# Sliding-window attention in five score units instead of six, with a relaid dense schedule

## The chip, the cores and the metric

The kernel runs on one core of a Trainium2 chip. The metric is device time in microseconds of one execution, as the median of several. A profile of one execution by the hardware profiler goes with it; its span runs from the first to the last instruction, and the execution's own time is a little longer than the span.

The engines are named as the profile names them: PE is TensorE (matrix products), PEld its weight loads, DVE is VectorE, ACT is ScalarE, POOL is GpSimd, and SP issues the DMA transfers from one queue (SPq).

## What is computed

A transformer block over 2048 tokens of width 512. A conditioning vector `c` gives six modulation rows (shift, scale and gate, twice). The first half is attention with 32 heads of width 16, in which a query sees its own and the 255 keys before it. The second half mixes tokens with an MLP over the sequence axis.

```python
mod = (silu(c) @ w_mod)            # six rows: sa, ca, ga, sb, cb, gb
h = layernorm(x) * (1 + ca) + sa
qkv = h @ wqkv                     # 32 heads, Dh = 16
scores = q @ k.T * Dh ** -0.5
mask = (0 <= i - j) & (i - j < 256)
o = softmax(where(mask, scores, -1e9)) @ v
x = x + ga * (o @ wo)
h = layernorm(x) * (1 + cb) + sb
u = gelu(einsum('sd,sf->df', layernorm(h), w1) + b1)   # S=2048, F=1792
x = x + gb * (u @ w2 + b2).T
```

## The kernel before

Tokens are cut into 16 blocks of 128, four blocks make a tile group (`tg` = 0 to 3), and the work has three parts: a short start up to the first scores, an attention loop over the four tile groups, and an MLP part in which TensorE works through W1, the GELU and W2.

**The attention loop.** Heads are taken four at a time (`hs` = 0 to 7; `g8 = hs // 2`, and `par` tells even from odd heads). TensorE runs four heads side by side in four 32-row strips of its array. One such set and one tile group needs 512 queries against up to 256 keys behind each of them, in blocks of 128 keys. A block of keys is fully or partly seen by 3 blocks of queries, so 12 blocks of 128 columns stand in 3 units of 512 columns (`UNITS`). A unit has four score banks of 512 columns, two `pss` tiles of two banks each. A loop step (`u`) does, in the order in which the code emits it:

- the exponential of the unit's first `pss` tile on ScalarE (`emit_exp(u, 0)`, L517), 1024 columns into bf16 `et`
- on TensorE the scores and masks of the next unit (`emit_scores(u + 1)`, L494 and L505); a mask is a small matmul that adds a huge negative number to what must not be seen. Three `pss` tiles exist, so its second tile takes the place of the one that the exponential just read
- on TensorE one "dense group" from a plan (`plan`), if the unit has one: Q, K or V projections of 4 matmuls of 512 columns, transposes of the normalised input, output projections, modulation rows or part of W1. It goes to one PSUM bank, the only buffer of `ps_dn`
- the exponential of the second tile (`emit_exp(u, 1)`)
- on VectorE pieces of LayerNorm and normalisation work from a list (`run_dve`), of which as many are taken as a planned budget per unit allows (2.0 us less what is queued), and then the emptying of the dense group
- on TensorE the products P·V of the unit before (`emit_av(u - 1)`, L533) into `po`, one bank. After the third unit of a set VectorE transposes `po` into `t2` (L547). Per pair of sets a reciprocal, a product and a transpose back follow (L556, L557, L564).

Every engine works in its own order of instructions; a standing instruction holds all behind it on its engine.

**K.** A projected K of a `g8` is cast into one buffer `ks` (L305), which `kspool` holds once. Eight small transfers (L315, 16 KB each) then spread its rows over two zeroed tiles, one per parity; the other parity's rows stay zero. The zeros come by DMA (`zeros`, L197). The next cast into `ks` waits until the eight transfers have landed. In the first tile group the first two `g8` are masked by VectorE instead.

**The plan.** In a unit number `ul` within the tile group (0 to 23), V is at 0 to 2, K of `g8` = 2 at 4 (5 in the first tile group), K of `g8` = 3 at 9, the next group's transposes at 11 to 14 and its first K's at 18 and 22. The budget's costs stand in the code beside each piece.

**Around it.** All of w_mod and the zeros are issued by SP's queue at the start; w1's first twelve row tiles are loaded in the second half of tile group 1 (from unit 16 on), the last four, and all of w2, after the loop. LayerNorm's two elementwise products (L591, L594) and the quotient (L557) run on VectorE.

Of the kernel before, what the change touches and what calls it, by code (L numbers as in the profile page):

```python
# [8 lines left out]
DT = mybir.dt  # L9
ACT = mybir.ActivationFunctionType  # L10
ALU = mybir.AluOpType
# [12 lines left out]
SCORE_SCALE = DH ** -0.5  # L24


@with_exitstack
def kernel(
# [61 lines left out]
    opool = ctx.enter_context(tc.tile_pool(name="opool", bufs=3))  # L90
# [31 lines left out]
    seed = modw.tile([32, 4 * P], DT.bfloat16, name="seed")  # L122
    seed_q = modw.tile([32, 2, 64], DT.bfloat16, name="seed_q")
    mask_k = const.tile([P, 4, P], DT.bfloat16, name="mask_k")
# [4 lines left out]
    def build_masks():  # L129
        v = nc.vector  # L130
        v.tensor_copy(
            out=spread[:].rearrange("p (a b) -> p a b", a=4),
            in_=identity[0:32, 0:32].unsqueeze(1).to_broadcast([32, 4, 32]),
        )
        bands = seed[:].rearrange("p (t x) -> p t x", t=2)
        for kind, (e0, e1) in enumerate(((-47, 0), (14, -33))):
            for lo in (0, 192):
                band = bands[:, kind, lo : lo + 64].rearrange("p (r s) -> p r s", s=2)
                v.memset(band[:, :, 0:1], 2.0 ** e0)
                v.memset(band[:, :, 1:2], 2.0 ** e1)  # L140
        v.memset(seed[:, 64:128], 2.0 ** 47)
        v.memset(seed[:, 128:192], 0.0)
        v.memset(seed[:, 320:384], 0.0)
        v.memset(seed[:, 384:448], 2.0 ** 14)
        for kind, (e0, e1) in enumerate(((14, -33), (0, 47))):
            q = seed_q[:, kind, :].rearrange("p (r s) -> p r s", s=2)
            v.memset(q[:, :, 0:1], -(2.0 ** e0))
            v.memset(q[:, :, 1:2], -(2.0 ** e1))

        def select(ap, pattern, base, cm, fill):  # L150
            nc.gpsimd.affine_select(
                out=ap, in_=ap, pattern=pattern, compare_op=ALU.is_ge, fill=fill, base=base, channel_multiplier=cm,
            )

        for lo in (0, 192):
            band = bands[:, :, lo : lo + 64]
            select(band, [[0, 2], [1, 64]], 0, -2, 0.0)
            select(band, [[0, 2], [-1, 64]], 1, 2, 0.0)
        select(seed[:, 64:128], [[0, 64]], -31, 1, 0.0)
        select(seed[:, 384:448], [[0, 64]], 0, -1, 0.0)  # L160
        select(seed_q[:, 0, :], [[1, 64]], 0, -2, -(2.0 ** 61))
        select(seed_q[:, 0, :], [[-1, 64]], 1, 2, 0.0)
        select(seed_q[:, 1, :], [[1, 64]], 0, -2, 0.0)
        select(seed_q[:, 1, :], [[-1, 64]], 1, 2, -(2.0 ** 47))
# [10 lines left out]
    epool = tc.alloc_tile_pool(name="epool", bufs=3)  # L175
# [20 lines left out]
    def zeros(r, g0=0):  # L196
        dma.dma_start(  # L197
            out=Kring[r][:, g0:].rearrange("p g n t -> p (g n) t"),
            in_=zero[:].unsqueeze(1).to_broadcast([P, 2 * (ND - g0), 4 * P]),
        )  # L200

    zeros(0, 2)
    zeros(1)
    for v in (2, 4, 3, 5):
        dma.dma_start(out=wmod[:, :, v * D : (v + 1) * D], in_=w_mod_v[:, :, v * D : (v + 1) * D])
    dma.dma_start(out=wod[:], in_=wo_v[:])
# [35 lines left out]
    def transpose_group(tg, dc, pool, act=False):  # L242
        def mms():
            if dc == 0:
                h1T[tg] = hpool.tile([P, ND, 4 * P], DT.bfloat16, name="h1T")
            pt = pool.tile([P, 4 * P], DT.bfloat16, name="dn")
            for tl in range(4):
                nc.tensor.transpose(
                    pt[:, tl * P : (tl + 1) * P], xn1[tg, tl][:, dc * P : (dc + 1) * P], identity[:]
                )  # L250
            return pt

        def evac(pt):
            if act:
                nc.scalar.activation(
                    out=h1T[tg][:, dc, :], in_=pt[:], func=ACT.Identity,
                    bias=modFM[:, dc : dc + 1], scale=modFM[:, 4 + dc : 5 + dc],
                )
            else:
                nc.vector.tensor_scalar(  # L260
                    out=h1T[tg][:, dc, :], in0=pt[:], scalar1=modFM[:, 4 + dc : 5 + dc],
                    scalar2=modFM[:, dc : dc + 1], op0=ALU.mult, op1=ALU.add,
                )
        return mms, evac, 0.6

    def v_group(tg, tl, pool, act=False):
# [15 lines left out]
        return mms, evac, 0.7  # L282
# [35 lines left out]
    def bc_group(v, dst, add1, pool):  # L318
# [9 lines left out]
        def evac(ps_b):  # L328
            if add1:
                nc.vector.tensor_scalar_add(out=dst[:], in0=ps_b[:], scalar1=1.0)  # L330
            else:
                nc.vector.tensor_copy(out=dst[:], in_=ps_b[:])
        return mms, evac, 0.7
# [14 lines left out]
    def wo_group(tb, pool):  # L348
# [19 lines left out]
    UNITS = (  # L368
        ((-1, 1, 2, 0), (-2, 2, 1, 2), (0, 0, 1, 3)),
        ((0, 1, 2, 0), (1, 0, 2, 2)),  # L370
        ((1, 2, 1, 0), (3, 0, 1, 1), (2, 0, 2, 2)),
    )

    FAR = ((1, 3), (1, 2), (0, 1))
    DIAG = ((3, 4), (2, 3), (1, 3))

    def MASKS(tg, ui):
        far = [] if (tg, ui) == (0, 0) else [(1, FAR[ui])]
        return [(0, DIAG[ui])] + far

    with tc.manual_schedule():

        with tc.tile_pool(name="modps", bufs=1, space=bass.MemoryType.PSUM) as modps, tc.tile_pool(
# [30 lines left out]
            nc.tensor.matmul(rows[:], lhsT=spread[:], rhs=seed[:], start=True, stop=True)  # L414
            nc.scalar.activation(out=mask_k[:].rearrange("p a b -> p (a b)"), in_=rows[:], func=ACT.Copy)
# [49 lines left out]
            evac(mms())  # L465
            nc.vector.tensor_copy(out=sT_rep[:], in_=sT[:].unsqueeze(2).to_broadcast([P, ND, P]))
# [8 lines left out]
        units = [(tg, hs, ui) for tg in range(NG) for hs in range(8) for ui in range(3)]  # L475
        state = {}

        def pieces(tg, ui):
            return [(4 * tg + kb, r0, nr, blk) for kb, r0, nr, blk in UNITS[ui] if 4 * tg + kb >= 0]

        def emit_scores(u):

            tg, hs, ui = units[u]
            g8, par = hs // 2, hs % 2
            pss = [ps_s.tile([P, 2, 4 * P], DT.float32, name="pss") for a in range(2)]
            state[u, 0], state[u, 1] = pss
            for n, (kb, r0, nr, blk) in enumerate(pieces(tg, ui)):
                Ksel = (KeT if par == 0 else KoT)[kb // 4][g8]  # L490
                k0, q0 = kb % 4 * P, (kb + r0 - 4 * tg) * P
                for j in range(4):
                    rows = slice(32 * j, 32 * j + 32)
                    nc.tensor.matmul(  # L494
                        pss[j // 2][:, j % 2, blk * P : (blk + nr) * P],
                        lhsT=Ksel[rows, k0 : k0 + P], rhs=QT[tg][g8][rows, q0 : q0 + nr * P],
                        start=(n == 0), stop=False,
                        tile_position=(32 * j, 0), skip_group_check=True,
                    )
            masks = [(lo, hi, kind, half) for kind, (lo, hi) in MASKS(tg, ui) for half in range(2)]  # L500
            for n, (lo, hi, kind, half) in enumerate(masks):
                for j in range(4):
                    rows = slice(32 * j, 32 * j + 32)
                    out = pss[j // 2][:, j % 2, lo * P : hi * P].rearrange("p (b q) -> p b q", q=P)
                    nc.tensor.matmul(  # L505
                        out[:, :, 64 * half : 64 * half + 64], lhsT=mask_k[rows, 2 * kind + half, :],
                        rhs=mask_q[rows, kind, :].unsqueeze(1).to_broadcast([32, hi - lo, 64]),
# [419 lines left out]
```

## Time and profile before

The three runs took 296.57, 298.05 and 298.37 us.

| | us |
|---|---|
| median of the runs | 298.05 |
| profiled execution, and its span | 297.41, 295.7 |
| first exponential starts | 15.01 |
| last exponential ends | 197.23 |
| start of the exponentials of tile groups 0, 1, 2, 3 | 15.0, 59.3, 105.0, 151.2 |
| busy in the span: PE, DVE, ACT, POOL | 260.1, 189.0, 191.4, 37.6 |
| from 130 to 160 us, of 30: PE, DVE, ACT, POOL | 25.2, 26.6, 29.2, 5.3 |

A row of the page's groups reads: line, engine, operation, what it writes and reads with the shapes, how often; busy time and mean ns of one; the idle time of the engine just before and what ended most of it. Busy time counts overlapping instructions once. A row of the order of time gives the start, the length until the last instruction of the row ended, the engine and line, how many were merged, and in brackets the idle time before the first and what ended it. The matmuls of a row are pipelined: a matmul's duration is longer than the step from one to the next.

### The profile page before, as it was taken

The page shows a single profiled execution, that of the slowest core. Times are in us where ns is not written, and L with a number is a line of the kernel's source. Part 1 is how long each engine was busy: PE and PEld are TensorE (multiplying, and loading weights), DVE is VectorE, ACT ScalarE, POOL GpSimd, SP SyncE. Part 2 cuts the span into 40 slices and gives each one's busy share as a digit, 9 for nine tenths or more (in the row PEclk, how much of TensorE's full clock was granted, in tenths as well). Part 3 has the DMA queues.
Part 4 walks back from the last instruction along what each step waited for, and adds up shares of the span by engine and source line. Part 5 has one row for each costly group of instructions (what it writes and reads, how often), then busy time and mean ns, then how long its engine had stood idle before and what let it go on. Part 6 is the DMA issues. An engine that isn't in the chain of part 4 may idle for free.

```text
span 295.7 us, 9616 instructions
## 1 busy us (share of the span) xinstructions
PE 260.1 (88%) x4182; PEld 132.9 (45%) x4232; DVE 189.0 (64%) x406; ACT 191.4 (65%) x222; POOL 37.6 (13%) x99
## 2 busy tenths in 40 slices
PE   6888588789889989888889888989999999999994
PEld 2444254445454544454444444544444444444441
DVE  6577393567895898998888788997911100505263
ACT  7678768999999989999999999963008121000000
POOL 6120020000110130131221031323510000000000
PEclk9999977999999999999999999999999999999999
DMA  6979513000003077300000000049960000012031
GB/s 187 324 242 317 163 48 117 20 22 8 16 20 129 21 265 259 142 21 2 14 22 8 21 11 12 4 158 395 412 279 3 0 0 2 24 48 72 2 104 38
DMA packets 21567, 29.22 MB, mean 99 GB/s; under 512 B 4116, under 2 KB 17684, under 8 KB 21524
## 3 DMA queue, kind: packets, MB, share of 16 engines
q1 hardware_dynamic: 21524, 28.59, 29.0%
q8 instruction: 33, 0.54, 0.7%
q14 instruction: 10, 0.08, 0.1%
HBM read 22.03 MB, written 2.10 MB: 82 GB/s over the span
## 4 chain that ended last, share of the span: by engine, by line
PE 55%; DVE 17%; ACT 9%; SPq 8%; DMA 7%; issue 3%; DVEq 0%
PE py L882 16%; ACT et L517 9%; PE pu L775 7%; PE pu L862 7%; PE pss L494 5%; PE dn L290 5%; PE po L533 4%; DMA wod<-in_A_wo_dram 3%; DVE t L547 3%; PE dn L270 3%; PE pss L505 2%; PE dn L625 2%; DVE x L363 2%; DVE ln_stats L574 2%; DVE ks L305 2%
## 5 line engine op out<-in xcount | busy, mean ns | idle before, releaser
L517 ACT ACTIVATE et<-pss 128x1024 bf16<-128x1024 f32 (+1 forms) x192 | 168.8, 1012 | 13.5 <-PE pss L505 12.9
L494 PE MATMUL pss<-QT,KT 32*128 32x256 bf16 (+1 forms) x960 | 44.8, 248 | 8.5 <-ACT et L517 8.0
L882 PE MATMUL py<-guT,w2r 128*128 128x512 bf16 x220 | 48.3, 379 | 0.2
L533 PE MATMUL po<-et,VaugT 128*32 128x256 bf16 (+1 forms) x960 | 37.8, 251 | 4.2 <-DVE t L547 3.5
L889 DVE SCALAR_TENSOR_TENSOR o<-py,bFM,bc_gb 128x512 bf16<-128x512 f32 x16 | 11.4, 746 | 44.4 <-PE py L882 44.4
L290 PE MATMUL dn<-h1T,wqkv 128*128 128x512 bf16 x112 | 31.4, 378 | 3.9 <-DVE x L363 1.4
L533 PEld LDWEIGHTS <-VaugT 128*32 128x32 bf16 x960 | 16.7, 95 | 39.3 <-issue 37.3
L882 PEld LDWEIGHTS <-w2r 128*128 128x128 bf16 x224 | 21.9, 98 | 26.5
L505 PE MATMUL pss<-mask_q,mask_k 32*128 32x64 bf16 (+1 forms) x1472 | 33.4, 199 | 0.0
L494 PEld LDWEIGHTS <-KT 32*128 32x128 bf16 x960 | 19.5, 93 | 27.9 <-issue 23.7
L216 POOL TENSOR_SCALAR ln_ve<-ln_mv 128x1 f32<-128x1 f32 (+1 forms) x40 | 9.8, 245 | 174.6 <-DVE ln_mv L576 92.6
L505 PEld LDWEIGHTS <-mask_k 32*128 32x128 bf16 x1472 | 28.7, 95 | 0.4
L220 POOL TENSOR_TENSOR ln_rstd<-ln_ve,mhalf 128x1 f32<-128x1 f32 (+1 forms) x40 | 24.5, 612 | 3.3
L547 DVE STREAM_TRANSPOSE t<-po 128x512 f32<-128x512 f32 x32 | 22.6, 706 | 1.4 <-PE po L533 1.4
L305 DVE CAST ks<-dn 128x512 bf16<-128x512 f32 x16 | 11.0, 689 | 13.0 <-DMA KT<-ks 6.7
L270 PE MATMUL dn<-wqkv,h1T 128*128 128x512 bf16 x56 | 16.6, 393 | 2.4 <-DVE VaugT L281 1.6
L290 PEld LDWEIGHTS <-wqkv 128*128 128x128 bf16 x128 | 10.9, 96 | 12.7 <-issue 3.0
L775 PE MATMUL pu<-hb,w1a 128*128 128x512 bf16 x70 | 15.9, 379 | 0.1
L281 DVE CAST VaugT<-dn 128x512 bf16<-128x512 f32 x15 | 10.3, 687 | 8.1 <-PE dn L270 7.4
L302 DVE CAST QT<-dn 128x512 bf16<-128x512 f32 x15 | 10.3, 687 | 6.7 <-PE dn L290 6.5
L862 PE MATMUL pu<-hb,w1a 128*128 128x512 bf16 x62 | 14.4, 379 | 0.1
L355 PE MATMUL dn<-wod,OTd 128*128 128x512 bf16 x39 | 11.9, 379 | 2.2 <-DVE ks L305 1.7
(106 smaller groups left out, 249.6 us busy)
## 6 DMA issues: line engine op xcount, KB each, us to landing
w2r<-in_B_w_dram SPq DMA_DIRECT2D x14, 512.0 KB, 10.2
w1a<-in_B_w_dram SPq DMA_DIRECT2D x12, 448.0 KB, 5.5
wmod<-in_w_mod_dram SPq DMA_DIRECT2D x6, 512.0 KB, 8.9
x<-in_A_x_dram SPq DMA_DIRECT2D x16, 128.0 KB, 3.8
KT<-zero SPq DMA_DIRECT2D x2, 1024.0 KB, 6.0
out_dram<-otile SPq DMA_DIRECT2D x16, 128.0 KB, 1.7
KT<-ks SPq DMA_DIRECT2D x112, 16.0 KB, 1.8
w1b<-in_B_w_dram SPq DMA_DIRECT2D x4, 448.0 KB, 4.2
```

The lines of the kernel that those rows point to most:

```text
L220: nc.gpsimd.tensor_tensor(out=r[:], in0=ve[:], in1=mhalf[:, 0:n], op=ALU.pow)
L270: nc.tensor.matmul(pv[:], lhsT=h1T[tg][:, dc, tl * P : (tl + 1) * P], rhs=wqkv[:, dc, 2 * D : 3 * D], start=(dc == 0), stop=(dc == ND - 1),)
L290: nc.tensor.matmul(pq[:], lhsT=wqkv[:, dc, col0 : col0 + P], rhs=h1T[tg][:, dc, :], start=(dc == 0), stop=(dc == ND - 1),)
L305: nc.vector.tensor_copy(out=ks[:], in_=pq[:])
L494: nc.tensor.matmul(pss[j // 2][:, j % 2, blk * P : (blk + nr) * P], lhsT=Ksel[rows, k0 : k0 + P], rhs=QT[tg][g8][rows, q0 : q0 + nr * P], ...
L505: nc.tensor.matmul(out[:, :, 64 * half : 64 * half + 64], lhsT=mask_k[rows, 2 * kind + half, :], rhs=mask_q[rows, kind, :].unsqueeze(1).to ...
L517: nc.scalar.activation(out=et[:, 2 * a : 2 * a + 2, b0 * P :], in_=state.pop((u, a))[:, :, b0 * P :], func=ACT.Exp, scale=SCORE_SCALE,)
L533: nc.tensor.matmul(po[32 * j : 32 * j + 32, q0 : q0 + nr * P], lhsT=VaugT[kb // 4][:, kb % 4, 8 * g8 + 2 * j + par, :], rhs=et[:, j, blk * ...
L547: nc.vector.transpose(out=state["t2"][:, hs % 2, :], in_=state["po"][:])
L775: nc.tensor.matmul(pu[:, i, :], lhsT=w1_of(sc, fc), rhs=hb[sc][:], start=(sc == 0), stop=(sc == NT - 1),)
L862: nc.tensor.matmul(pu[:, i, :], lhsT=w1_of(sc, fc), rhs=hb[sc][:], start=(sc == s0), stop=(sc == NT - 1),)
L882: nc.tensor.matmul(pys[tl][:], lhsT=w2r[:, fc, tb * P : (tb + 1) * P], rhs=guT[fc][:], start=(fc == 0), stop=(fc == NF - 1),)
```

## The change

Twelve blocks of 128 columns per set are laid out anew. The first 64 queries of a block see only the lower 64 keys of their own block, and the last 64 queries see only the upper 64 keys of the block two back. These outer parts need half of the partitions each, and the change puts them into one shared unit.

- A set of four heads gets two units of its own (kind A, 4 per pair of sets) of 512 columns. Both parities share a unit of kind C: its lower 64 partitions hold the own block's first 64 keys against its first 64 queries, its upper 64 partitions the last 64 keys of the block two back against its last 64 queries. So a pair of sets takes 5 units (`KINDS`: A, C, A, A, A), the loop 80 instead of 96, and the exponentials 160 instead of 192.
- C's scores are 64 matmuls of 64 columns and its masks 8 of 512 columns, in strips of 32 rows by 64 columns. Its P·V are two bursts per set (lower and upper halves) of 16 matmuls of 64 columns in strips of 64 rows by 32 columns. [...]
- The output of C's exponentials has a pool of its own (`cpool`, three half tiles), A's has six half tiles.
- The plan is laid over 20 units per tile group. K of `g8` = 2 and 3 are at 4 and 6 in every tile group, the next group's K at 12 and 15 (tile group 0) or 13 and 17. The budget per unit is 1.9 us (1.5 in the two short units of tile group 0). Transposes go two columns at a time.
- GpSimd does the quotient product and the two LayerNorm products of the loop, and the zeros of K as memsets. In tile group 0 ScalarE empties the V groups and three modulation rows.
- A second V group is done before the loop; four pieces of w_mod and wo are loaded at units 5 to 9 of tile group 0; eleven of w1's row tiles are loaded from unit 2 of tile group 1, five after the loop. `opool` has two buffers instead of three.

The diff, cut to its core:

```diff
-    opool = ctx.enter_context(tc.tile_pool(name="opool", bufs=3))
+    opool = ctx.enter_context(tc.tile_pool(name="opool", bufs=2))
...
-    epool = tc.alloc_tile_pool(name="epool", bufs=3)
+    epool = tc.alloc_tile_pool(name="epool", bufs=6)
+    cpool = tc.alloc_tile_pool(name="cpool", bufs=3)
...
-    zeros(0, 2)
-    zeros(1)
-    for v in (2, 4, 3, 5):
-        dma.dma_start(out=wmod[:, :, v * D : (v + 1) * D], in_=w_mod_v[:, :, v * D : (v + 1) * D])
-    dma.dma_start(out=wod[:], in_=wo_v[:])
+    def zeros(r, g):
+        nc.gpsimd.memset(Kring[r][:, g], 0.0)
...
+    A_PIECES = (
+        ((0, 64, 256, 0), (-2, 0, 64, 256), (-1, 0, 192, 320)),
+        ((3, 448, 64, 0), (2, 320, 192, 64), (1, 192, 256, 256)),
+    )
+    KINDS = (("A", 0, 0), ("C", 0, None), ("A", 0, 1), ("A", 1, 0), ("A", 1, 1))
...
+            mms, evac, _ = v_group(0, 1, hps)
+            evac(mms())
+            for g in (2, 3):
+                zeros(0, g)
...
+            for par in range(2):
+                for b in range(4):
+                    c0 = 256 * par + 64 * b
+                    own, far = 4 * tg + b, 4 * tg + b - 2
...
+                    for j in range(4):
+                        for half, kb in ((0, own), (1, far)):
...
+                            nc.tensor.matmul(
+                                pss[j // 2][64 * half : 64 * half + 64, j % 2, c0 : c0 + 64],
+                                lhsT=keys(kb, g8, par)[rows[j], k0 : k0 + 64], rhs=QT[tg][g8][rows[j], q0 : q0 + 64],
+                                start=(par, b) == (0, 0), stop=False, tile_position=(32 * j, 64 * half),
+                                skip_group_check=True,
+                            )
...
+            et = (epool if kind == "A" else cpool).tile([P, 2, 4 * P], DT.bfloat16, name="et")
...
+        def emit_av(u):
+            tg, g8, k = units[u]
+            if k != 1:
+                av_a(tg, g8, k)
+            if k == 1 or k == 3:
+                state["lo"] = av_c(tg, g8, k // 2, 0)
+
+        def close_head_set(tg, g8, par, behind):
+            av_c(tg, g8, par, 1, behind)
+            norm_out(par)
...
-                nc.vector.tensor_tensor(
+                nc.gpsimd.tensor_tensor(
                     out=m[:].rearrange("p (b a d) -> p a b d", a=2, d=DH), in0=t2v[:, :, :, 0:DH],
...
-            return [(quotient, 1.15, 0), (back, 0.7, 0)]
+            return [(quotient, 0.4, 1), (back, 0.7, 0)]
...
-                nc.vector.tensor_tensor(out=v["h2"][:], in0=v["h2"][:], in1=bc_cb1[:], op=ALU.mult)
+                nc.gpsimd.tensor_tensor(out=v["h2"][:], in0=v["h2"][:], in1=bc_cb1[:], op=ALU.mult)
+                nc.gpsimd.tensor_tensor(out=v["h2"][:], in0=v["h2"][:], in1=bc_sb[:], op=ALU.add)
...
-            own = ((3, 1, "k"), (4, 1, "q"), (5, 2, "k"), (6, 2, "q")) if tg == 0 else (
-                (3, 1, "q"), (4, 2, "k"), (5, 2, "q"))
-            for ul, g8, kind in own + ((8, 3, "q"), (9, 3, "k")):
+            own = ((2, 1, "q"), (3, 1, "k"), (4, 2, "k"), (5, 2, "q"), (6, 3, "k"), (7, 3, "q")) if tg == 0 else (
+                (3, 1, "q"), (4, 2, "k"), (5, 2, "q"), (6, 3, "k"), (8, 3, "q"))
+            for ul, g8, kind in own:
                 lay(ul, qk_group(tg, g8, kind, ps_dn))
...
+                t0, t1, k0, v0, q0, k1, v1 = (10, 11, 12, 13, 14, 15, 16) if tg == 0 else (11, 12, 13, 15, 16, 17, 18)
...
+            if tg == 0:
+                if 1 <= ul <= 4:
+                    zeros(1, ul - 1)
+                if 5 <= ul <= 8:
+                    zeros(2, ul - 5)
+                    v = (4, 2, 5, 3)[ul - 5]
+                    dma.dma_start(out=wmod[:, :, v * D : (v + 1) * D], in_=w_mod_v[:, :, v * D : (v + 1) * D])
...
-            if tg == 1 and ul == 16:
+            if tg == 1 and ul == 2:
...
+            behind = emit_exp(u, 0)
             if u + 1 < len(units):
                 emit_scores(u + 1)
+            closes = (units[u - 2][0], units[u - 2][1], 1) if k == 1 and u > 1 else (tg, g8, 0) if k == 4 else None
+            if closes:
+                close_head_set(*closes, behind)
...
+        turn = small.tile([P, 1], DT.float32, name="turn")
+        memset = nc.vector.memset(turn[:], 0.0).ins
+        tc.add_manual_dep(memset, state["lo"].name, IN_TURN, reason="row tiles of one PSUM bank")
+        close_head_set(NG - 1, ND - 1, 1, memset)
```

## The prediction

> **What bounds it now.** I read the page's groups first, then the waits, then the order of time inside the attention loop. The exponentials come first.
>
> ```profile
> L517 ACT ACTIVATE et<-pss 128x1024 bf16<-128x1024 f32 (+1 forms) x192 | 168.8, 1012 | 13.5 <-PE pss L505 12.9
> L557 DVE TENSOR_TENSOR merge<-t,zr 128x512 bf16<-128x512 f32 x16 | 11.1, 691 | 0.6
> L505 PE MATMUL pss<-mask_q,mask_k 32*128 32x64 bf16 (+1 forms) x1472 | 33.4, 199 | 0.0
> ```
>
> They run from 15.01 us to 197.23 us: 182.2 us, of which ScalarE computes 168.8 and idles 13.5, nearly all of it waiting for scores. Inside that stretch, the timeline of TensorE in the third tile group (tg = 2), and one unbroken run of ScalarE:
>
> ```profile
> 113.05 0.40 PE L494 MATMUL pss<-QT,KT 32*128 32x256 bf16 x8
> 113.28 0.28 PE L505 MATMUL pss<-mask_q,mask_k 32*128 32x64 bf16 x16
> 113.57 1.02 PE L290 MATMUL dn<-h1T,wqkv 128*128 128x512 bf16 x3
> 114.52 0.41 PE L533 MATMUL po<-et,VaugT 128*32 128x128 bf16 x12
> ...
> 114.86 0.40 PE L494 MATMUL pss<-QT,KT 32*128 32x128 bf16 x12
> ```
> ```profile
> 82.67 10.19 ACT L517 ACTIVATE et<-pss 128x1024 bf16<-128x1024 f32 x11 [0.61 <-PE pss L505]
> ```
>
> Eleven exponentials in 10.19 us, the last 1.02 long: one starts every 0.91 us, a unit costs ScalarE 1.82. TensorE needs, from start to start, 0.52 for scores and masks (113.05 to 113.57), 0.95 for a dense group, 0.34 for the P·V products: 1.81. Both engines are at the limit in a unit with a dense group. A tile group's floor is 24 x 1.82 = 43.7; the groups with tg of 1 to 3 measure 45.7 to 46.1.
>
> A second limit hides in the copies of K. They leave one buffer (`ks`) in eight small transfers from SP's queue:
>
> ```profile
> 26.34 0.69 DVE L305 CAST ks<-dn 128x512 bf16<-128x512 f32 x1 [1.04 <-PE dn L290]
> ...
> 36.34 0.69 DVE L305 CAST ks<-dn 128x512 bf16<-128x512 f32 x1 [3.61 <-DMA KT<-ks]
> ```
> ```profile
> 38.27 0.66 ACT L517 ACTIVATE et<-pss 128x256 bf16<-128x256 f32 x2 [2.21 <-PE pss L505]
> ```
>
> The second cast stood 3.61 us, until the first one's transfers had landed, 10.0 us after that cast began. Behind it VectorE empties nothing, the one dense PSUM buffer stays full, TensorE stands at its next dense group, and ScalarE ran dry for 2.21 us. Of such a wait about 1.4 us is absorbed. Other casts began 7.5 us (51.50 to 58.99) and 10.3 us (69.69 to 79.97) behind one that they waited for.
>
> **The five units, part by part.** For four heads of each parity the old kernel had 6 units, now 5: 12 exponentials become 10, 10.9 us become 9.1. Over 16 such sets this takes away 32 exponentials, 29 us. Three things stand against it.
>
> TensorE. Four A units: 512 score columns and 256 mask columns in 24 matmuls; the old unit of the same columns took 0.52 with 28, I take 0.50. P·V stays 0.34. The shared C unit adds 64 score matmuls of 64 columns and 8 masks of 512. The nearest row is the run of 16 masks of 64 columns above: 0.28 less the 0.19 of the last, over 15, 6 to 7 ns each: 64 make 0.45, the masks (two halves side by side, 0.22 for 512 columns by the 0.216 step of the dense matmuls) 0.2, the switch of shape 0.1: 0.75. Bounds: 0.55 if eight run at once throughout, 2.1 if the two halves of a row group go in turn (32 pairs of 0.03, then five steps of 0.216). Its P·V is four bursts per set, each 16 matmuls of 64 columns, four at a time: 4 x 27 ns plus the 0.12 of a switch (0.34 less 512 columns at 0.216): 0.23, at most 0.33 if narrow weights slow it.
>
> Now the order. Call 0 the start of C's first exponential. It ends at 1.05. TensorE does the next scores (to 1.55), then closes the previous set with the upper halves (to 1.78). C's exponentials share three buffers, two per unit, so the second one overwrites the buffer that this closing has just read: it can start at 1.9, not at 0.91. **One us is lost in every set.** The third unit's first exponential is at 2.8, then 4.65, 6.45, 8.3. In the last unit TensorE has scores, closing, dense group, P·V and a lower burst: 0.50 + 0.23 + 0.95 + 0.34 + 0.23 = 2.25, from 7.5 to 9.75; then C's scores end at 10.4, seen by ScalarE at 10.6 instead of 10.1. So a set takes 10.6, against 11.5 measured. A tile group is 42.6 with the closing's other waits. In tg = 0 two units have half the columns (0.48 by the 0.27 of 256 and the 0.91 of 1024), but every unit has a dense group and five evacuations (V twice, modulation rows three times) go to ScalarE at half a step, 5 x 0.46: 40.8. Sum 168.6, 13.6 less than now, from the loop's own order.
>
> **The relaid dense groups.** K of g8 = 2 stays at unit 4, K of g8 = 3 moves from 9 to 6: two units apart instead of five (in tg = 0 from 5 and 9 to 4 and 6). From cast to cast pass the rest of unit 4, 0.57, unit 5, 2.04, and unit 6 up to its dense group's end, 1.9: 4.5 us. The transfers need 7.5 to 10.3; I take 8.0 in tg = 2 and 3, 9.5 in tg = 1, where SP's queue now carries a 448 KB piece of w1 in each unit from 2 on, 8.5 in tg = 0, where the pieces of w_mod follow directly. VectorE stands 3.5, 3.5, 5.0 and 4.0; less the absorbed 1.4: 2.1 + 2.1 + 3.6 + 2.6. In tg = 0 K of the next group comes at 12 and 15, three units of 2.0 apart: 2.5 less 1.4, 1.1. At 13 and 17 the distance is four units, 8.5, and I take nothing. Together 11.5. Queued behind the standing cast are the transposes of `po`, the LayerNorm pieces and the next evacuation; these make what is late next. The loop kept 2.4 us per tile group above its floor; VectorE loses work, so I keep 1.0 of it per group: 4.
>
> **GpSimd's products.** Sixteen quotient and 24 norm products leave VectorE: 16 x 0.691 and 12 x (0.425 + 0.406), 21 us, worth nothing unless VectorE binds. GpSimd's time for one is in no row: at least the 0.52 of its 128x512 memset, at most three of these for two reads and a write, 1.6; I take 1.0. The cover is the gap of one or two units that the planner leaves; without it each late quotient would hold VectorE's back transpose by up to 1.6. Ten memsets of K (1.05 each, twice the row) replace 2.5 MB of zero transfers at the start, and w_mod's last four pieces come later. That removes the SP crowd behind the 10.0 us above; I have credited it in 8.5. The bias and modulation rows otherwise have their units' cover. If piece 4 lands after unit 9 starts (SP has 8 copies and a piece of 1.2 before it, 5.6, and a piece takes up to 8.9 to land), up to 4 us; I take 0 and keep it for the range.
>
> **Start and end.**
>
> ```profile
> 13.46 1.02 PE L270 MATMUL dn<-wqkv,h1T 128*128 128x512 bf16 x4
> ...
> 13.97 0.42 DVE L466 COPY sT_rep<-sT 128x512 bf16<-128x512 bf16 x1
> ...
> 14.41 0.10 PEld L494 LDWEIGHTS <-KT 32*128 32x128 bf16 x4 [0.42 <-DVE sT_rep L466]
> ```
>
> A second V group now stands ahead of the loop: four more matmuls (0.86) behind those of 13.46, its cast (0.69), then the copy that the first scores waited for: 1.7 later after 0.2 saved by smaller masks. At the end the memset that keeps the last halves in turn and the quotient on GpSimd (1.0 for 0.69, a hop more) add 0.7; two tiles of dense matmuls, 2.6 us, cover the rest. Eleven instead of twelve early w1 tiles and two instead of three output buffers: nothing, since TensorE reads the fifth late tile over 10 us after the loop; if that cover failed, one tile's 4.2 us landing.
>
> **The sum.** 168.6 + 11.5 + 4 = 184.1 against 182.2: +1.9; +1.7 and +0.7: +4.3. The profiled execution took 297.4 (span 295.7 and 1.7 around), 0.6 below the median 298.05: 301.7, or 302.4 on the median's footing. The pieces late behind a standing VectorE come on top with half a us: **303**. The unknowns of this case alone give 297 to 311.
>
> **Rivals.**
> *The K copies don't hold.* If they land in about 4.5 us, no cast waits; 11.5 vanish: 291. They decide the sign at about 6.5 us. For it: SP is freed of the zeros and, at the start, of w_mod. Against: no waited-for pair is under 7.5. With the C buffer's wait gone too, another 11 to 12: 279. Chances 0.20 and 0.07.
> *C's narrow matmuls go in turn.* At 1.5 instead of 0.75, 16 x 0.75 = 12 more: 315; from 1.0 on it decides over any gain. For it: no row has two column halves in one row group. Against: four column strips of P·V start within 10 ns of each other. Chance 0.10. [...]
> *GpSimd stops VectorE.* If each product holds VectorE for its 1.0, twelve in a tile group make 35 us of work (41 in the third group now, 90% of 46, less 6) into 47, longer than the group: about 1.5 more in each: 309. Against: without that, a quarter of VectorE is idle. Chance 0.08. [...]
>
> **Chances.** Forecast 0.55. Within 1% is what a measurement tells from no change, 295 to 301: a quarter of the forecast and a little of the first rival, 0.17. Below: the first rival and a little of the forecast, 0.26. Above: 0.57. The range leaves out the 279 and the tail of the narrow matmuls: 286 to 315.
>
> **What would show it.** 160 exponentials; a step of about 1.9 us from the first to the second exponential of each C unit, with `po` matmuls ending between; casts of `ks` with 3 to 5 us behind KT<-ks at unit 6; C's 72 matmuls in 0.65; GpSimd products near 1.0. Wrong would make it: copies landing within 5 us, or ScalarE with enough scores ahead to swallow both waits.

## The result, and the profile after

The changed kernel takes 324.18 us (median; 323.84 to 325.37) against 297.31 (295.45 to 298.37) for the kernel before on the same chip: a ratio of 1.092, with a 95% interval of 1.085 to 1.099. The profiled execution took 324.23 (span 322.4), 26.8 more than the profiled one of before. The sign was forecast, the size was not: the sum gave +4.3.

Where the time went can be read from ScalarE's exponentials, from the first to the last:

| us | before | after | difference |
|---|---|---|---|
| first exponential starts | 15.01 | 15.28 | +0.3 |
| attention loop | 182.2 | 207.4 | +25.1 |
| last exponential's end to the end of the span | 98.5 | 99.8 | +1.3 |
| mean granted TensorE clock, whole span | 0.988 | 0.942 | |

So the loop holds nearly all of it. The groups of the page after, in the form line, engine, operation, tiles and count, then busy us and mean ns, then the idle time before and what ended most of it:

```profile
L533 ACT ACTIVATE et<-pss 128x1024 bf16<-128x1024 f32 (+1 forms) x160 | 145.2, 996 | 52.4 <-PE pss L495 20.3
...
L599 POOL TENSOR_TENSOR merge<-t,zr 128x512 bf16<-128x512 f32 x16 | 17.0, 1060 | 68.8 <-DVE zr L598 68.8
...
L288 DVE CAST ks<-dn 128x512 bf16<-128x512 f32 x16 | 11.1, 692 | 22.4 <-DMA KT<-ks 18.0
L495 PE MATMUL pss<-mask_q,mask_k 32*128 32x64 bf16 (+1 forms) x736 | 21.2, 204 | 0.0
```

The exponentials did shrink as the change says, from 192 to 160 and by 23.6 us of busy time. ScalarE's idle time ahead of them grew by 38.9, from 13.5 to 52.4. The waits of the same run name three enders of that idle time (the columns are the total, how often, and the longest):

```profile
ACT et L533 <- PE pss L495: 20.3, 13, 4.7
DVE ks L288 <- DMA KT<-ks: 18.0, 5, 4.5
...
ACT et L533 <- PE po L564: 15.1, 15, 1.2
...
ACT et L533 <- PE pss L520: 12.7, 14, 2.5
...
PE dn L338 <- DVE ks L288: 10.7, 3, 3.9
```

L495 ends an A unit's scores, L520 a C unit's, and L564 is the closing burst (the P·V of a set's upper halves, in `close_head_set`) that the second exponential of a C unit waits for. The line of `ks` is the wait for K's copies: 18.0 us in five waits, where the prediction had five of 3.5, 3.5, 5.0, 4.0 and 2.5, which is 18.5. The sums agree better than their parts: in order of time the waits are 2.31, 4.46, 3.20, 3.80 and 4.25 us, where 4.0, 2.5, 5.0, 3.5 and 3.5 were forecast.

**One such wait, closely.** It stands at unit 6 of the third tile group. In order of time, first VectorE, then ScalarE, then TensorE of the changed kernel (start, length, engine and line, merged count, and in brackets the idle time before and its ender):

```profile
142.20 0.69 DVE L288 CAST ks<-dn 128x512 bf16<-128x512 f32 x1 [3.80 <-DMA KT<-ks]
```
```profile
137.02 4.69 ACT L533 ACTIVATE et<-pss 128x1024 bf16<-128x1024 f32 x5 [1.17 <-PE po L564]
145.99 1.94 ACT L533 ACTIVATE et<-pss 128x1024 bf16<-128x1024 f32 x2 [4.29 <-PE pss L495]
```
```profile
139.16 0.35 PE L495 MATMUL pss<-mask_q,mask_k 32*128 32x128 bf16 x10
142.94 1.87 PE L338 MATMUL dn<-wod,OTd 128*128 128x512 bf16 x4 [3.42 <-DVE ks L288]
144.74 0.40 PE L564 MATMUL po<-et,VaugT 64*32 64x64 bf16 x16
145.07 0.61 PE L487 MATMUL pss<-QT,KT 32*128 32x64 bf16 x12
```

VectorE stands 3.80 us, TensorE stands 3.42 behind it, and ScalarE 4.29: longer than the wait that causes it. Behind the other four waits, in order of time, ScalarE stands 4.18, 3.81, 4.23 and 4.74 us, so that the five cost it 21.3 us for 18.0 us of waits. What adds to it is seen in the table of stretches. Its columns are the stretch, its length, the busy time (and count) of PE, PEld, DVE, ACT and POOL, the granted clock, the DMA share and GB/s.

```profile
128.00:138.00 10.00, 8.46 (x268) 4.59 (x270) 8.06 (x15) 7.95 (x10) 3.58 (x6) 1.00 0.03 8
138.60:142.90 4.30, 0.51 (x22) 0.46 (x22) 0.70 (x2) 3.10 (x4) 0.71 (x1) 0.90 0.07 19
142.90:148.20 5.30, 5.26 (x62) 1.89 (x63) 2.92 (x6) 1.94 (x2) 3.08 (x4) 0.50 0.09 24
148.20:158.00 9.80, 8.53 (x297) 5.51 (x294) 7.46 (x16) 7.29 (x8) 4.14 (x5) 0.97 0.02 5
```

For 5.3 us after the stand the granted clock is 0.50 (the whole slow stretch runs from 142.0 to 148.9, so it starts within the stand). The four dense matmuls at 142.94 take 1.87 us, 0.41 from one to the next (1.87 less the last one's 0.64, by three), where the prediction counted 0.216 and the page after has 48.5 us for L937's 224. This stand is followed by more than two units of a TensorE at half its speed, which at full speed is already at the limit (1.81 of a unit's 1.82 us, by the rows of before). The page's clock row shows the same in tenths, first before, then after:

```profile
PEclk9999977999999999999999999999999999999999
```
```profile
PEclk9999769799969999987999795999999999999999
```

The two slow slices of before come after that kernel's own 3.61-us wait, the one from which the prediction took its price. TensorE's five stands behind `ks` are 2.64, 2.65, 3.36, 3.42 and 3.88 us, with 10.2, 3.4, 6.8, 6.8 and 6.8 us at 0.50, and another 3.4 us at 0.50, from 179.6 on, have no such stand ahead of them. So here the length of a stand alone doesn't tell whether or for how long the clock is halved.

### The profile page after: what moved, and what is told of

Same layout as the page of the kernel before. It is cut to its first block, busy times and chain, and to the rows that moved or that the text cites. A ratio compares the mean times of both kernels' runs of the same rounds, so it can differ in the third digit from the quotient of the medians.

```text
span 322.4 us, 11390 instructions
## 1 busy us (share of the span) xinstructions
PE 275.3 (85%) x5096; PEld 135.9 (42%) x5096; DVE 170.3 (53%) x355; ACT 170.1 (53%) x195; POOL 89.4 (28%) x145
## 4 chain that ended last, share of the span: by engine, by line
PE 64%; ACT 9%; SPq 8%; DVE 8%; DMA 5%; issue 3%; POOL 1%; DVEq 0%; ACTq 0%; POOLq 0%
PE py L937 15%; ACT et L533 8%; SPq L298 8%; PE dn L273 7%; PE pu L830 6%; PE pu L917 6%; PE pss L487 5%; PE dn L253 4%; PE po L544 3%; PE po L564 3%; DMA KT<-ks 3%; PE dn L338 3%; PE pss L512 2%; DMA w1a<-in_B_w_dram 2%; PE dn L666 2%
## 5 line engine op out<-in xcount | busy, mean ns | idle before, releaser
L533 ACT ACTIVATE et<-pss 128x1024 bf16<-128x1024 f32 (+1 forms) x160 | 145.2, 996 | 52.4 <-PE pss L495 20.3
L487 PE MATMUL pss<-QT,KT 32*128 32x192 bf16 (+2 forms) x704 | 33.9, 250 | 17.2 <-ACT et L533 14.9
L937 PE MATMUL py<-guT,w2r 128*128 128x512 bf16 x224 | 48.5, 380 | 0.0
L273 PE MATMUL dn<-h1T,wqkv 128*128 128x512 bf16 x128 | 37.3, 420 | 3.2 <-DVE ks L288 2.6
L599 POOL TENSOR_TENSOR merge<-t,zr 128x512 bf16<-128x512 f32 x16 | 17.0, 1060 | 68.8 <-DVE zr L598 68.8
L937 PEld LDWEIGHTS <-w2r 128*128 128x128 bf16 x224 | 21.9, 98 | 26.4
L590 DVE STREAM_TRANSPOSE t<-po 128x512 f32<-128x512 f32 x32 | 22.9, 716 | 17.4 <-PE po L564 17.2
L544 PE MATMUL po<-et,VaugT 128*32 128x192 bf16 (+2 forms) x704 | 26.5, 253 | 2.5 <-DVE t L590 2.5
L487 PEld LDWEIGHTS <-KT 32*128 32x128 bf16 x704 | 14.6, 95 | 32.1 <-issue 27.2
L495 PE MATMUL pss<-mask_q,mask_k 32*128 32x64 bf16 (+1 forms) x736 | 21.2, 204 | 0.0
L564 PE MATMUL po<-et,VaugT 64*32 64x64 bf16 x960 | 19.3, 197 | 0.4 <-DVE VaugT L264 0.4
L495 PEld LDWEIGHTS <-mask_k 32*128 32x128 bf16 x736 | 18.4, 99 | 0.6
L632 POOL TENSOR_TENSOR h<-h,bc_cb 128x512 bf16<-128x512 bf16 x12 | 13.9, 1155 | 10.0 <-DVE h L621 10.0
```

The lines of the kernel that those rows point to most:

```text
L273: nc.tensor.matmul(pq[:], lhsT=wqkv[:, dc, col0 : col0 + P], rhs=h1T[tg][:, dc, :], start=(dc == 0), stop=(dc == ND - 1),)
L487: nc.tensor.matmul(pss[j // 2][:, j % 2, c0 : c0 + nq], lhsT=keys(kb, g8, par)[rows[j], k0 : k0 + P], rhs=QT[tg][g8][rows[j], q0 : q0 + nq ...
L495: nc.tensor.matmul(pss[j // 2][:, j % 2, c0 : c0 + 64 * nb].rearrange("p (b q) -> p b q", q=64), lhsT=mask_k[rows[j], P * what : P * what ...
L533: act = nc.scalar.activation(out=et[:, :, 0:n], in_=state.pop((u, a))[:, :, 0:n], func=ACT.Exp, scale=SCORE_SCALE,)
L544: nc.tensor.matmul(state["po"][32 * j : 32 * j + 32, q0 : q0 + nq], lhsT=VaugT[kb // 4][:, kb % 4, 8 * g8 + 2 * j + par, :], rhs=state["e" ...
L564: mm = nc.tensor.matmul(state["po"][32 * j : 32 * j + 32, q0 : q0 + 64], lhsT=VaugT[kb // 4][part64, kb % 4, 8 * g8 + 2 * j + par, :], rhs ...
```

## The experiments

The quoted expectations weigh two theories. In short, A puts most of the loss on the waits for K's copies, with the slow stretch behind them; B leaves those at about the predicted price and looks for the rest in the sets themselves. All ratios are against the kernel before on the same chip, and a difference between two experiments is one of their ratios, times 298.

**e1: the changed kernel with one early w1 tile less.** The next ones need a little room for a second buffer, and this one shows what making the room costs.

```diff
-NA = 11
+NA = 10
```

> The changed kernel with ten instead of eleven early row tiles of w1 and six late ones, which frees room for the next three kernels; the computation is the same. Both theories: no change from 324.2 (323 to 326), since the sixth late tile is read more than 8 us after the loop.

Measured: 325.94 us, ratio 1.093 (1.084 to 1.102). That is the changed kernel's own ratio. One stray execution of 1296 us is left out of the ratio. All experiments but e5 (which edits the kernel before) and e9 contain this edit, and it costs nothing that can be seen.

**e2: two buffers for `ks`.** The cast of K no longer waits for the transfers of the cast before it.

```diff
-    kspool = tc.alloc_tile_pool(name="kspool", bufs=1)
+    kspool = tc.alloc_tile_pool(name="kspool", bufs=2)
```

> As the one before, with two buffers for the cast of K (kspool), so that no cast waits for the transfers of the last one. Theory A (the five waits of 3.6 us each cost 4.4 us of ScalarE's idle time at once and about 1 us more in the next units, since TensorE's clock falls while it stands): 27 us less, 297 (292 to 302), and a granted clock back near 0.98. Theory B (the prediction's own account, a wait less 1.4 us absorbed; the rest of the loss is in the C units and the products on GpSimd): 11 us less, 313.

Measured: 304.94 us, ratio 1.024 (1.020 to 1.029). That is 20 us less (1.0927 less 1.0243, times 298). From the page of this run:

```profile
PEclk9799969999999899799999999999999999999999
...
L533 ACT ACTIVATE et<-pss 128x1024 bf16<-128x1024 f32 (+1 forms) x160 | 144.8, 999 | 35.5 <-PE po L564 15.2
...
L288 DVE CAST ks<-dn 128x512 bf16<-128x512 f32 x16 | 11.0, 689 | 8.2 <-PE dn L273 7.5
```

No cast waits more than 0.22 us for a transfer any more. ScalarE's idle time falls by 16.9, most of the slow slices are gone, and the loop is 186.8. The five waits and what they drag along were worth 20 us: 18.0 us of waits, with nothing absorbed and about 0.5 us each on top, instead of 11.5. That lies between the two theories, a little nearer to A's number and outside A's range: the price is of A's kind, but it doesn't explain all of the loss.

**e3: four buffers for C's exponentials instead of three** (on e1). The second exponential of a C unit no longer waits for the closing burst.

```diff
-    cpool = tc.alloc_tile_pool(name="cpool", bufs=3)
+    cpool = tc.alloc_tile_pool(name="cpool", bufs=4)
```

> As the first, with four instead of three buffers for the exponentials of the C units (cpool), so that the second exponential of a C unit does not wait for the closing of the set before. Theory A (the 15 gaps of 1.1 us are time lost at ScalarE, but TensorE is what ends the sets next): 10 to 15 less, 309 to 314; the gap from first to second exponential of a C unit falls to 0.91. Theory B (TensorE ends every set anyway and the gap is only idle time moved): under 4 us less, 320 to 324.

Measured: 321.22 us, ratio 1.077 (1.070 to 1.085): 5 us less than e1 (0.0155 times 298), with intervals that allow 1 to 8. That is between the two theories, near B's 4. The wait that it takes away is 15.1 us by the row of after; in this run's trace no exponential waits for L564. So two thirds of what ScalarE gained was lost again behind another engine.

**e4: both together.**

> Both added buffers. Theory A: the two gains add, 324 less 27 less 12 is 285 (278 to 292), faster than the kernel before. Theory B: 313 less 4 is 309, so that the five units lose to six even without both waits, through the C units' many small matmuls and the products on GpSimd.

Measured: 299.29 us, ratio 1.0025 (0.999 to 1.007): the time of the kernel before, midway between the two theories (285 and 309). On top of e2 the buffer is worth 6.5 us (0.0218 times 298), of 15.2 us of waits. The five-unit set with both waits gone is as fast as the six-unit set with its own. The eight exponentials that each tile group saves, 29 us in all, buy nothing at this point.

**e5: the kernel before, with only the spacing of the K casts changed.** K of `g8` = 3 goes to two units behind K of `g8` = 2, as in the change; what stood in that unit goes to unit 9. Everything else, six units and VectorE's products, is the kernel before.

```diff
-            for ul, g8, kind in own + ((8, 3, "q"), (9, 3, "k")):
+            for ul, g8, kind in own + ((8, 3, "q"), (7 if tg == 0 else 6, 3, "k")):
...
-        WO = {0: (), 1: (17, 19, 21, 23), 2: (6, 10, 15, 19), 3: (6, 7, 10, 12)}
+        WO = {0: (), 1: (17, 19, 21, 23), 2: (9, 10, 15, 19), 3: (7, 9, 10, 12)}
```

> The kernel before with one edit of its plan: K of the last pair of heads (g8 = 3) two units behind K of g8 = 2, as the change has it, at 7 in tile group 0 and at 6 in the others; what stood at 6 goes to 9. Nothing else moves. Theory A (a wait costs 4.4 us at once and 1 us more behind it, cold clock with it): four new or longer waits, 16 to 22 more, 316 (312 to 320), casts of ks 3 to 4.5 us behind KT<-ks, and a lower granted clock. Theory B (a wait less 1.4 absorbed): 4 x 2 to 3, 307.

Measured: 319.62 us, ratio 1.078 (1.069 to 1.087): +21.6 us over its 298.03. The page and the waits of this run:

```profile
PEclk9599755999789999979999998999999999999999
...
L517 ACT ACTIVATE et<-pss 128x1024 bf16<-128x1024 f32 (+1 forms) x192 | 168.9, 1010 | 32.8 <-PE pss L505 32.1
```
```profile
ACT et L517 <- PE pss L505: 32.1, 22, 6.9
...
DVE ks L305 <- DMA KT<-ks: 21.0, 5, 5.0
```

The waits for the copies grow by 14.3 us (21.0 from 6.7), ScalarE's idle time by 19.3 (32.8 from 13.5), the execution by 21.6. In the profiled executions 2.3 of this lie ahead of the first exponential (17.3 us for 15.0), where the edit does nothing, and the loop is 19.5 us longer. So the spacing, with the pieces that made room for it, costs on the six-unit kernel, without GpSimd's products, what e2 gives back on the changed one. This is the run that ties the loss to the spacing, and its price is 1.4 us of the loop per us of added wait. Theory A's range for this run, 312 to 320, holds the result; theory B's 307 lies far below.

**e6: the three products of GpSimd back on VectorE** (on e4). The order of the code and the budgets of the plan stay.

```diff
-                nc.gpsimd.tensor_tensor(
+                nc.vector.tensor_tensor(
...
-                nc.gpsimd.tensor_tensor(out=v["h2"][:], in0=v["h2"][:], in1=bc_cb1[:], op=ALU.mult)
-                nc.gpsimd.tensor_tensor(out=v["h2"][:], in0=v["h2"][:], in1=bc_sb[:], op=ALU.add)
+                nc.vector.tensor_tensor(out=v["h2"][:], in0=v["h2"][:], in1=bc_cb1[:], op=ALU.mult)
+                nc.vector.tensor_tensor(out=v["h2"][:], in0=v["h2"][:], in1=bc_sb[:], op=ALU.add)
```

> The changed kernel with both added buffers, and the quotient product and the two LayerNorm products back on VectorE, in the same order and under the same planned costs. [...] If TensorE and ScalarE set the end, VectorE only gets 20 us more to do in 182, and the time stays within 2 us, or rises a little where an evacuation comes later.

Measured: 318.99 us, ratio 1.070 (1.058 to 1.083): 20 us more than e4. The expectation missed by far. VectorE, then TensorE, in the third tile group of this run:

```profile
145.49 0.35 DVE L598 RECIPROCAL zr<-t 128x32 f32<-128x32 f32 x1
145.88 0.69 DVE L599 TENSOR_TENSOR merge<-t,zr 128x512 bf16<-128x512 f32 x1
146.49 0.41 DVE L621 TENSOR_SCALAR hb<-h,ln_mv,ln_rstd 128x512 bf16<-128x512 bf16 x1
146.81 0.99 DVE L243 TENSOR_SCALAR h1T<-dn,modFM 128x512 bf16<-128x512 bf16 x2
```
```profile
147.86 1.03 PE L235 MATMUL dn<-identity,xn 128*128 128x128 bf16 x8 [1.50 <-DVE h1T L243]
```

The quotient and a LayerNorm piece stand ahead of the emptying of the dense bank, since the plan still counts the first at 0.4 us, where its two rows take 1.04, and gives the second its old room. The emptying at 146.81 comes late, and TensorE stands 1.50 us for the single dense buffer. The run's granted clock is 0.944, and ScalarE's idle time before the exponentials is 42.4. So under this plan VectorE does bind, by when it empties the bank and not by its busy share. What this run doesn't show is the cost under a plan that counts the products as VectorE's; that wasn't tried.

**e7: w_mod's four pieces and wo loaded before the loop, and Q of `g8` = 1 one unit earlier in the last three tile groups** (on e4). These are two edits, and the run doesn't part them.

```diff
+    for v in (4, 2, 5, 3):
+        dma.dma_start(out=wmod[:, :, v * D : (v + 1) * D], in_=w_mod_v[:, :, v * D : (v + 1) * D])
+    dma.dma_start(out=wod[:], in_=wo_v[:])
...
-                (3, 1, "q"), (4, 2, "k"), (5, 2, "q"), (6, 3, "k"), (8, 3, "q"))
+                (2, 1, "q"), (4, 2, "k"), (5, 2, "q"), (6, 3, "k"), (8, 3, "q"))
```

> The changed kernel with both added buffers, with w_mod's four late pieces and wo loaded ahead of the loop, where the kernel before has them, and Q of g8 = 1 at unit 2 instead of 3 in tile groups 1 to 3 (its cast ended after TensorE wanted it). Theory A: the wait of TensorE for a piece of w_mod at unit 9 of tile group 0, 2.5 us and half the clock behind it, and three waits of 0.45 go: 5 less, 294. Theory B (tile group 0 is slow because every unit has a dense group): at most 1 less, 298.

Measured: 294.68 us, ratio 0.988 (0.984 to 0.992): 4.2 us less than e4 (0.0142 times 298), and 1.2% less than the kernel before. The wait that the first edit removes can be seen in e2's trace, at unit 9 of the first tile group; it was not in the sum:

```profile
ACT et L533 <- PE pss L520: 14.5, 14, 5.0
...
PE dn L305 <- DMA wmod<-in_w_mod_dram: 2.6, 1, 2.6
```

The 5.0 in the first row is ScalarE's stand behind that wait: the granted clock is 0.50 from 39.9 to 46.8 us there, though TensorE stands only 2.6.

In e7's page the clock row has one slow slice outside the start, and ScalarE idles 22.9 us before the exponentials:

```profile
PEclk9799999999999799999999999999999999999999
...
L537 ACT ACTIVATE et<-pss 128x1024 bf16<-128x1024 f32 (+1 forms) x160 | 145.7, 982 | 22.9 <-PE pss L524 12.4
```

**e8: C's 64 score matmuls replaced by 8 of 512 columns** (on e4). It scores the wrong keys, so part of the computation is changed: the column count on TensorE is the same for each strip, and only the number of instructions differs.

```diff
-            for par in range(2):
-                for b in range(4):
...
+            for j in range(4):
+                for half in range(2):
+                    nc.tensor.matmul(
+                        pss[j // 2][64 * half : 64 * half + 64, j % 2, :],
+                        lhsT=keys(4 * tg, g8, half)[rows[j], 0:64], rhs=QT[tg][g8][rows[j], :],
```

> The changed kernel with both added buffers, in which the C unit's 64 score matmuls of 64 columns are 8 of 512 columns; it scores the wrong keys, so its output is not the reference's, and everything behind it runs as it is. If the many small matmuls make C's first exponential late (0.75 us lost in each of 16 units), their 0.50 us become about 0.2 and the time falls by 4 to 5 us from 299. If the long step ahead of C (scores, closing, dense group, two bursts) makes it late, 0 to 2 us.

Measured: 292.47 us, ratio 0.985 (0.977 to 0.992): 5.4 us less than e4 (0.018 times 298; the intervals allow 3 to 8), 0.3 us per C unit, as the first of the two expectations has it. The order of time on TensorE says where: a C unit of the changed kernel, then one of this run.

```profile
161.53 0.71 PE L512 MATMUL pss<-QT,KT 32*64 32x64 bf16 x64
162.04 0.47 PE L520 MATMUL pss<-mask_q,mask_k 32*64 32x512 bf16 x8
162.44 1.04 PE L253 MATMUL dn<-wqkv,h1T 128*128 128x512 bf16 x4
```
```profile
149.63 0.42 PE L504 MATMUL pss<-QT,KT 32*64 32x512 bf16 x8
149.87 0.40 PE L511 MATMUL pss<-mask_q,mask_k 32*64 32x512 bf16 x8
```

From the first score to the first mask pass 0.51 us with 64 matmuls and 0.24 with 8: the 0.3 by which a set gets shorter. From the first score to the next dense group pass 0.91 (162.44 less 161.53), 0.51 for the scores and 0.40 for the masks and the switch of shape.

**e9: the changed kernel, with only the plan's K moved back.** K of `g8` = 3 returns to unit 9 in the last three tile groups, still with one `ks` and three C buffers; three of the five long waits should go.

```diff
-                (3, 1, "q"), (4, 2, "k"), (5, 2, "q"), (6, 3, "k"), (8, 3, "q"))
+                (3, 1, "q"), (4, 2, "k"), (5, 2, "q"), (9, 3, "k"), (8, 3, "q"))
...
-            for ul in {0: (), 1: (7, 9, 10, 14), 2: (7, 9, 10, 14), 3: (7, 9, 10, 11)}[tg]:
+            for ul in {0: (), 1: (6, 7, 10, 14), 2: (6, 7, 10, 14), 3: (6, 7, 10, 11)}[tg]:
```

> The changed kernel, one buffer for the cast of K as it has it, with only its plan edited in tile groups 1 to 3: K of g8 = 3 at unit 9 again, five behind K of g8 = 2, and the output projection of 9 at 6. If the distance of two units makes the waits, three of the five go without any added buffer, three fifths of the 20 us that the second buffer took away: 312 (309 to 316). If the second buffer helped in another way, less than 4.

Measured: 313.1 us; its four executions are 306.59, 312.77, 313.43 and 314.59, so no interval is given. The long waits in tile groups 1 to 3 are gone from the trace: two of 3.3 and 4.8 us are left, both in the first tile group. The fall is 10 to 18 us below the changed kernel, with the 12 that three fifths of e2's 20 would be inside it. So the spacing makes these waits in the new layout too, without a new buffer; the price of one can't be told from so wide a spread.

**e10: K of `g8` = 2 one unit earlier** (on e7), into the unit that e7 left without a dense group, so that unit 4 is free for what is late.

```diff
-                (2, 1, "q"), (4, 2, "k"), (5, 2, "q"), (6, 3, "k"), (8, 3, "q"))
+                (2, 1, "q"), (3, 2, "k"), (5, 2, "q"), (6, 3, "k"), (8, 3, "q"))
```

> As e7_early, with K of g8 = 2 at unit 3 instead of 4 in tile groups 1 to 3, so that unit 4, which closes a set and runs a lower burst, has no dense group. If the long step ahead makes C's first exponential late, three of sixteen gaps of 0.7 go: 2 us less, 292.5. If C's own matmuls do: within 1 of e7's 294.7.

Measured: 294.61 us, ratio 0.994 (0.990 to 0.999). e7 has 294.68 and 0.988 on another chip: no gain that can be told. That speaks for C's own matmuls, as e8 does, and against the long step ahead of them.

## Why the prediction was right or wrong

**The step that failed: "Of such a wait about 1.4 us is absorbed."** This term is 9 of the 23 us by which the loop was off; the other 14 stand below under the set's own order, and they alone would have brought the time to the range's upper end. The waits came at the units named, and their sum was right (18.5 forecast, 18.0 measured), though by luck: single waits were off by up to 2.0 us to either side. The price on them was wrong: "Together 11.5" is 20 by e2, and 19.5 in the loop by e5 on the kernel before alone. The 1.4 came from one row, a wait of 3.61 with an idle time of 2.21 on ScalarE behind it, and that reading stopped too early. The same trace shows the rest of the bill. The transposes of `xn` in the units that follow that wait and some units later, and two stretches of the same time in a table as above:

```profile
39.97 0.61 PE L248 MATMUL dn<-identity,xn 128*128 128x128 bf16 x4
...
43.49 0.40 PE L248 MATMUL dn<-identity,xn 128*128 128x128 bf16 x4
```
```profile
39.20:42.60 3.40, 3.40 (x76) 2.34 (x72) 3.27 (x8) 2.34 (x3) 0.92 (x2) 0.50 0.11 29
42.60:46.00 3.40, 2.60 (x67) 1.51 (x67) 2.67 (x6) 3.02 (x6) 0.92 (x2) 1.00 0.71 232
```

The same four matmuls took 0.61 and 0.40, at a granted clock of 0.50 and 1.00. In the slow stretch ScalarE was busy for 2.34 of 3.40 us; its 1.06 of idle time and the 2.21 ahead of it are nearly the whole wait of 3.61. The prediction showed the wait and not the stretch behind it. Besides, that wait fell in the first tile group, beside short units (exponentials of 256 columns), which may be why ScalarE lost so little at once; in the changed kernel four of the five waits cost ScalarE more at once than their own length. How much of the 20 is the stand and how much the half clock is not parted by these runs, but they bound it. With a mean granted clock of 0.942 over 322.4 us and of 0.971 over e2's 303.0 the clock that isn't granted falls from 18.7 us to 8.8, by 9.9; TensorE's five stands sum to 16.0. Neither reaches 20, so as an estimate the half clock has 4 to 10 of the 20 us.

**"I take 0" for the piece of w_mod at unit 9.** TensorE stood 2.6 us for it in e2, and ScalarE 5.0. Its removal, with an earlier Q, gave 4.2; the stated bound was "up to 4".

**The set's own order, 168.6 and 4 for hiccups.** Without waits for K the loop should have been 172.6 and was 186.8 in e2, 14 longer. By tile group e2 has 50.9, 45.7, 45.4 and 44.9 us, where 41.8 and three times 43.6 were forecast, hiccups included: 9 of the 14 lie in the first tile group, which the prediction had as the shortest. Some 4 to 5 of that is the piece of w_mod. "**One us is lost in every set**" held: 15.2 us in 15 waits for the closing burst in e2, 1.0 each. C's scores and masks take 0.9 instead of 0.75, 16 x 0.15 = 2.4. Also too small is C's late first exponential, "10.6 us instead of 10.1", 16 x 0.5 = 8: the waits for C's scores are 14.5 in e2, or 9.5 without the longest, 5.0, which is that of w_mod. And the terms that stood beside each other as a sum were not independent: when the 15 us of the C buffer went (e3, e4), only 5 to 6.5 came back. TensorE ends the sets next. The rival with both waits gone, 279, is therefore refuted by e4 at 299.3. The remainder of the 14 us, some 7, was not traced to single units, and its cause stays open.

**"21 us, worth nothing unless VectorE binds".** The durations were right: 1060 ns for the quotient, and the norm products

```profile
L632 POOL TENSOR_TENSOR h<-h,bc_cb 128x512 bf16<-128x512 bf16 x12 | 13.9, 1155 | 10.0 <-DVE h L621 10.0
```

against 1.0 forecast. That they are worth nothing doesn't hold under this plan: with the products back on VectorE and the plan's costs as they are, 20 us are lost (e6).

**The rivals.** *The K copies don't hold*: refuted, the casts waited 18.0 us in all. *C's narrow matmuls go in turn*: refuted. They start within 0.51 us, 8 ns apart, against 0.45 forecast. The unit up to the next dense group takes 0.9, against 0.75 forecast and 1.5 in the rival; the term that was short is the masks with the switch of shape, 0.40 for 0.3. By e8 the small matmuls cost some 0.3 us a unit more than large ones. The 0.33 that the prediction allows a burst of P·V "if narrow weights slow it" rests on no run: in the changed kernel a burst takes 0.23 us from its start to the next matmul (161.30 to 161.53), as forecast. *GpSimd stops VectorE*: seen as longer instructions beside its products, and small. VectorE beside two of GpSimd's products:

```profile
128.44 2.47 DVE L221 TENSOR_SCALAR xn<-x,ln_mv,ln_rstd 128x512 bf16<-128x512 bf16 x4
```
```profile
127.74 1.15 POOL L632 TENSOR_TENSOR h<-h,bc_cb 128x512 bf16<-128x512 bf16 x1
128.96 1.15 POOL L633 TENSOR_TENSOR h<-h,bc_sb 128x512 bf16<-128x512 bf16 x1
```

Four of these normalisations take 2.47 us, when a lone one takes 0.40: the first two take 0.59 and 1.31, and in e6, without the products, the same four take 0.37 to 0.41 each; in the kernel before, a pair takes 0.73. Three of L621 beside products take 0.59 to 1.15. The excess over 0.40 is 2.2 us for these five. (Two more, of 1.01 and 1.11 us, run beside K's memsets ahead of the loop.) The price is near 2 us of VectorE's time in the loop, where the rival had 6 us of the total (309 for 303). Why VectorE is slower beside a product was not shown.

**Start and end.** "1.7 later" was 0.3 in the profiled execution; the variants of the changed kernel began between 15.3 (e6, e10) and 17.0 (e4), and e5, a variant of the kernel before, at 17.3, so this term is not settled. The end took 1.3 instead of 0.7. **The exponentials** were 160, and their 0.91 step held (0.92 in the run of five from 137.02).

**The sum again.** 11.5 became 20.6 (207.4 less e2's 186.8) and 172.6 became 186.8: 184.1 became 207.4, 23.3 us more. Start and end were 0.8 under their terms (0.3 and 1.3 for 1.7 and 0.7), which gives the 22.5 between the forecast +4.3 and the measured +26.8. That e2, with 304.94, lies near the forecast 303 is luck: there the waits are gone and the set's own order is 14 too long. The range ended at 315. It had the w_mod piece and a narrow C in it, and no bound on the price of a wait, which was treated as known since a row showed it.

**What stays open.** Stand and half clock were not parted (a kernel that keeps TensorE busy during a wait was not tried). Nor was a plan for e6's kernel that counts VectorE's products at their true cost. In e7 the loop is 175.5 us where 160 exponentials at 0.91 would take 145.6; of the 30 us between, 22.9 are ScalarE's idle time ahead of exponentials, nearly all in small waits for TensorE's scores, and the rest is ScalarE's other work with the waits for it.

## What to carry to other kernels

Before moving two uses of a single buffer closer together, measure in the trace how long the slowest transfer out of it takes, and compare it with the new distance in time, not in steps; a second buffer of 1 KB per partition was worth 20 us here. Price a stand of a bound engine with all that follows it, to the point where its instructions have their usual durations again: here stands of 2.6 to 3.9 us had slow stretches of 3.4 to 10.2 us with them. And work that is taken off the busiest engine gains only what the next engine has to spare, so cost it by removing each wait in turn, not by adding the savings.

## What the runs showed of the hardware

- With a stand of 3.42 us TensorE's granted clock was 0.50 for 6.8 us, and a dense matmul's step 0.41 us instead of 0.216 (48.5 us for 224 on L937). A stand of 2.64 us had 10.2 us at 0.50 with it, and the slow stretches of the changed kernel's loop last 3.4, 6.8 or 10.2 us.
- Score matmuls with 32 rows and 64 columns of weights start 8 ns apart on average over eight tiles (64 in 0.51 us). In e8 eight of 512 columns, two column halves of four row groups, take 0.24 us to the next matmul, near the 0.216 of one: the two halves run side by side.
- A GpSimd product of 128x512 took 1.06 us from f32 and 1.15 us from bf16, and a memset of 128x1024 bf16 0.96 us; a VectorE normalisation that meets one takes up to 1.3 us instead of 0.40.
- Eight 16 KB transfers from one queue kept their source buffer busy from one cast to the next that waited: 7.5 to 10.3 us in the kernel before, 7.5 to 8.9 in the changed one.
